# Attention softmax split between ScalarE and VectorE: a five-bank score ring, VectorE's scores in side banks, PV of two key tiles at a time, more slots for P, and an instruction order built with a price for tiling-mode changes

## Chip, cores, metric

One core of a Trainium2 chip. The metric is the device time of one execution in microseconds (us); lower is better. A span is what the profile covers of an execution, some 2 us less than its time.

## The reference

Layer norm, then self-attention times a gated feed-forward network (FFN), plus a residual. All inputs are bf16; 2048 positions, width 448, 16 heads of 28, FFN width 1792.

```python
xn = _layernorm(x)
qkv = (xn @ wqkv).reshape(B, S, 3, H, Dh) ...            # H = 16, Dh = 28
p = softmax(einsum("bhqd,bhkd->bhqk", q, k) * Dh**-0.5)  # 16 x 2048 x 2048 exponentials
s = einsum("bhqk,bhkd->bhqd", p, v) ... @ wo
g = silu(gelu(xn @ w1 + b1) @ w2 + b2)
out = x + s * g
```

The scores are cut into 1024 tiles of 128 keys x 512 queries, 64 for each of 16 blocks (a block is one group of four heads and one quarter of the queries). Each tile needs an exponential of 512 columns.

## The kernel before

A builder in Python runs its own list of tasks and fixes, before anything is compiled, the order of every engine's instructions. For each task it has a duration, and it picks the task that can start first by its own reckoning. The chip then follows that order; only semaphores, not the reckoning, decide the times.

Scores go from TensorE into a ring of six PSUM banks, in units of three (two in the first block). ScalarE takes the exponential of a whole unit in one instruction and writes bf16 tiles P to SBUF; PV multiplies P by V. For some tiles VectorE does the exponential instead, with a conversion out of the bank and three polynomial steps in SBUF. Before, such a tile is the last of its ring unit, so the unit leaves ScalarE two banks:

```python
UNITS = [range(m, m + 2) ...] + [_seq[i:i + 3] ...]      # ring units
ms = UNITS[u][:-1] if K.pick_late(u) else UNITS[u]       # VectorE takes the last one
...
def fexp(eng, b0=b0, p0=p0, n=n):                        # ScalarE
    return eng.activation(K.P[:, p0:p0 + n, :], K.ring[:, b0:b0 + n, :], ACTF.Exp, scale=SM_SCALE)
...
yield _Task(DVE, ... eng.tensor_scalar(ysb, K.ring[:, RB[m], :], ...))   # VectorE, then three steps:
yield _Task(DVE, ... eng.scalar_tensor_tensor(u, lo, EXP_A, lo, op0=ALU.add, op1=ALU.mult))
yield _Task(DVE, ... eng.scalar_tensor_tensor(u, u, EXP_B, u, op0=ALU.add, op1=ALU.mult))
yield _Task(DVE, ... eng.scalar_tensor_tensor(pl, u, EXP_K, y, op0=ALU.mult, op1=ALU.add))
# [cut]
```

One bank (`misc`) is the side bank for all other products, one (`acc`) collects PV. In the middle of the run stands GELU: ScalarE changes its table, reads 35 FFN tiles that VectorE has put into SBUF before (`p_f1`) and 21 directly from the ring (`p_direct`), and changes the table back.

```python
yield ("until", lambda: K.exp_u >= GU and K.n_f1 == len(SBT))   # GELU: all 35 must be there
```

Whether VectorE takes a tile is decided by two tables for the 16 blocks, `THS` (how much work VectorE may have waiting) and `SLACKS` (how far past the end of the block's exponentials its work may reach). P has 21 slots. When TensorE would be busy less than 85% of the last 3.4 us by its reckoning, the builder adds groups of three warming matmuls that add zero to `acc`.

## Time and profile before

| | before |
|---|---|
| time, us: median at first (3 runs) | 475.94 |
| span of the profiled execution | 474.0 |
| ScalarE busy | 462.4 (98%) |
| VectorE busy | 379.2 (80%) |
| TensorE matmuls busy | 435.4 (92%), 145 warming groups of three among them |
| exponentials on ScalarE | 231 of three banks, 118 of two, 1 of one |
| tiles on VectorE | 94 |

ScalarE is the engine without a gap; TensorE's 92% includes warming work, and the ends of its matmuls are modelled in the trace. The lines are in the prediction below.

### The profile page before, as it was taken

To read this page: it belongs to the slowest core of one execution; us is meant where nothing else is said; L and a number is where in the kernel's file an instruction comes from. 1 tells how busy PE (TensorE), PEld (TensorE's weight loads), DVE (VectorE), ACT (ScalarE), POOL (GpSimd) and SP (SyncE) were. 2 spreads that over 40 slices of the span, in tenths; PEclk is the share of its full clock that TensorE was granted. 3 is DMA by queue.
4 is the path that set the end of the run, shared out by engine and by line. 5 is a ranking of instruction groups with operands and counts; after the bars stand their busy time and mean duration, and the time that the engine had idled before them with its cause. 6 is when DMAs were issued, how large, how long until landed. Compare 5 with 4: busy or idle time off the path is not lost.

```text
span 474.0 us, 9973 instructions
## 1 busy us (share of the span) xinstructions
PE 435.4 (92%) x4150; PEld 164.0 (35%) x4185; DVE 379.2 (80%) x550; ACT 462.4 (98%) x394; POOL 39.7 (8%) x78
## 2 busy tenths in 40 slices
PE   6999999999989898989989989999999999999995
PEld 4443333333322333332223442233333333332453
DVE  8946979889885978898895939895785969899875
ACT  6999999999999999999999999999999999999994
POOL 7370001000100001000100000000100101010001
PEclk9999999999999999999999999999999999999999
DMA  8401000000000000000300000000010101011011
GB/s 268 136 8 30 2 1 0 1 1 3 1 1 0 1 1 1 1 2 21 117 1 0 1 1 1 1 1 1 1 40 2 39 1 40 1 59 39 23 41 40
DMA packets 8287, 11.08 MB, mean 23 GB/s; under 512 B 1649, under 2 KB 6897, under 8 KB 8242
## 3 DMA queue, kind: packets, MB, share of 16 engines
q1 hardware_dynamic: 7954, 9.75, 6.6%
q8 instruction: 33, 0.54, 0.5%
q10 hardware_dynamic: 288, 0.69, 0.4%
q14 instruction: 12, 0.10, 0.1%
HBM read 8.61 MB, written 1.84 MB: 22 GB/s over the span
## 4 chain that ended last, share of the span: by engine, by line
ACT 43%; PE 38%; issue 13%; DVE 4%; DMA 1%; ACTq 0%; DVEq 0%
ACT P L1195 41%; PE ring L1156 11%; PE acc L1389 7%; PE misc L1092 5%; PE misc L1034 4%; PE acc L884 2%; PE misc L722 2%; ACT h L1071 2%; PE ring L1034 2%; PE misc L1480 1%; PE misc L976 1%; DMA x_sb<-in_A_x_dram 1%; PE ring L722 1%; PE ring L976 1%; DVE kT L1331 0%
## 5 line engine op out<-in xcount | busy, mean ns | idle before, releaser
L1195 ACT ACTIVATE P<-ring 128x1536 bf16<-128x1536 f32 (+1 forms) x350 | 420.5, 1467 | 0.6 <-PE ring L1156 0.3
L1156 PE MATMUL ring<-qT,kT 32*128 32x512 bf16 (+2 forms) x1144 | 136.4, 359 | 22.0 <-ACT P L1195 16.3
L1389 PE MATMUL acc<-P,vaug 128*32 128x512 bf16 (+2 forms) x1055 | 95.9, 362 | 0.3 <-issue 0.3
L1218 DVE TENSOR_SCALAR x_sb<-ring 128x512 f32<-128x512 f32 x86 | 59.2, 688 | 26.8 <-PE ring L1156 25.9
L1156 PEld LDWEIGHTS ring<-qT,kT 32*128 32x128 bf16 x1144 | 35.6, 91 | 130.0 <-ACT P L1195 119.7
L1092 PE MATMUL misc<-w,h 128*128 128x448 bf16 x224 | 51.7, 355 | 0.2 <-DVE w L1097 0.2
L1453 POOL CAST rhi<-rc 128x16 bf16<-128x16 f32 x15 | 10.4, 692 | 394.5 <-DVE rc L1451 296.1
L1389 PEld LDWEIGHTS acc<-P,vaug 128*32 128x32 bf16 x1055 | 24.8, 93 | 50.8 <-issue 45.1
L884 PE MATMUL acc<-ident,zero 128*128 128x128 bf16 x435 | 40.4, 221 | 0.0
L1034 PE MATMUL misc<-xnT,w 128*128 128x512 bf16 x128 | 36.2, 382 | 1.4 <-issue 0.8
L1017 DVE CAST h<-misc 128x512 bf16<-128x512 f32 x35 | 24.1, 688 | 10.8 <-PE misc L1034 10.6
L1331 DVE SCALAR_TENSOR_TENSOR kT<-x_sb 128x1024 f32<-128x1024 uint16 (+1 forms) x28 | 32.0, 1141 | 0.7
L884 PEld LDWEIGHTS acc<-ident,zero 128*128 128x128 bf16 x435 | 25.1, 97 | 20.5 <-issue 19.0
L1332 DVE SCALAR_TENSOR_TENSOR kT<-kT 128x1024 f32<-128x1024 f32 (+1 forms) x28 | 31.9, 1138 | 0.4
L1331 DVE SCALAR_TENSOR_TENSOR w<-x_sb 128x1024 f32<-128x1024 uint16 (+1 forms) x22 | 25.7, 1168 | 0.4
L1332 DVE SCALAR_TENSOR_TENSOR w<-w 128x1024 f32<-128x1024 f32 (+1 forms) x22 | 25.8, 1171 | 0.2
L1092 PEld LDWEIGHTS misc<-w,h 128*128 128x128 bf16 x224 | 17.5, 97 | 23.7 <-issue 11.5
L1034 PE MATMUL ring<-xnT,w 128*128 128x512 bf16 x82 | 19.7, 380 | 0.8 <-ACT h L1071 0.6
L1334 DVE SCALAR_TENSOR_TENSOR x_sb<-kT,x_sb 128x1024 uint16<-128x1024 f32 (+1 forms) x16 | 19.0, 1187 | 0.2
L1071 ACT ACTIVATE h<-h 128x2560 bf16<-128x2560 bf16 (+2 forms) x8 | 16.6, 2073 | 0.0
L733 DVE TENSOR_SCALAR kT<-misc,ecol 128x512 bf16<-128x512 f32 x13 | 9.7, 748 | 8.3 <-PE misc L722 8.1
L1334 DVE SCALAR_TENSOR_TENSOR x_sb<-w,x_sb 128x1024 uint16<-128x1024 f32 (+1 forms) x14 | 16.0, 1142 | 0.1
(158 smaller groups left out, 425.9 us busy)
## 6 DMA issues: line engine op xcount, KB each, us to landing
h<-in_A_x_dram SPq DMA_DIRECT2D x4, 448.0 KB, 3.3
w<-in_B_w_dram SPq DMA_DIRECT2D x1, 1568.0 KB, 7.1
w<-in_B_w_dram SPq DMA_DIRECT2D x1, 1344.0 KB, 8.7
out_dram<-h SPq DMA_DIRECT2D x6, 224.0 KB, 1.9
x_sb<-in_A_x_dram SPq DMA_DIRECT2D x2, 448.0 KB, 5.2
h<-in_A_wqkv_dram SPq DMA_DIRECT2D x3, 168.0 KB, 4.8
x_sb<-in_A_x_dram ACTq DMA_DIRECT2D x1, 448.0 KB, 4.4
out_dram<-h SPq DMA_DIRECT2D x4, 112.0 KB, 1.7
```

The source lines that it names most:

```text
L884: ins = eng.matmul(K.acc[:, 0:128], K.zero[:, :], K.ident[:, :], start=False, stop=True, skip_group_check=True)
L1017: yield _Task(DVE, lambda eng: eng.tensor_copy(dst, bank), [tok], wr, 0.69, 0.0, 2)
L1034: ins = eng.matmul(bank, K.w1[:, kt, ft * 128:(ft + 1) * 128], K.xnT[:, kt, c * 512:(c + 1) * 512], start=(kt == 0), stop=(kt == KT - 1))
L1071: yield _Task(ACT, lambda eng, dst=dst, src=src: eng.activation(dst, src, ACTF.Gelu_apprx_tanh), rd, K.b_hf[c][f0:f0 + n] + ([K.b_h[c]] if ...
L1092: ins = eng.matmul(ps, hv[:, ft, t * 128:(t + 1) * 128], K.w2[:, ft, :], start=(ft == 0), stop=(ft == FT - 1))
L1156: return eng.matmul(K.ring[:, RB[m], col:col + nq], K.kT[32 * j:32 * j + 32, g, t * 128:(t + 1) * 128], K.qT[32 * j:32 * j + 32, g, c * 51 ...
L1195: return eng.activation(K.P[:, p0:p0 + n, :], K.ring[:, b0:b0 + n, :], ACTF.Exp, scale=SM_SCALE)
L1218: yield _Task(DVE, lambda eng, m=m, i=i, half=half: eng.tensor_scalar(K.ysb[i][:, 512 * half:512 * half + 512], K.ring[:, RB[m], :], SM_SC ...
L1331: yield _Task(DVE, lambda eng: eng.scalar_tensor_tensor(u, lo, EXP_A, lo, op0=ALU.add, op1=ALU.mult), ty, [tu], d, 0.0, 4)
L1332: yield _Task(DVE, lambda eng: eng.scalar_tensor_tensor(u, u, EXP_B, u, op0=ALU.add, op1=ALU.mult), [tu], [tu], d, 0.0, 4)
L1334: yield _Task(DVE, lambda eng: eng.scalar_tensor_tensor(pl.bitcast(dt.uint16), u, EXP_K, y, op0=ALU.mult, op1=ALU.add), ty + [tu], [K.b_pl ...
L1389: return eng.matmul(K.acc[32 * j:32 * j + 32, q0:q0 + nq], K.vaug[:, t, 4 * g + j, :], ap[:, col:col + nq], tile_position=(0, 32 * j), sta ...
```

## The change

The intent: relieve ScalarE of more tiles. The ring becomes five banks (units of three and two in turn) and the bank saved becomes a second side bank. VectorE's scores go to a side bank, in one group of matmuls with a ring unit's. PV takes two key tiles (eight tiles of P) at once. Free parts of `h` and `xnT` become extra P slots (42 in all before GELU, 36 after). The builder's durations are set to nearer values, and a change between full, row-tiled and column-tiled matmuls costs 0.1 us in it. The diff, cut to its core:

```diff
-        for u in range(NU):
-            ms = UNITS[u]
+        while K.next_m < MTOT:
+            b0 = 4 * (u % 2)
+            n = 2 if b0 or K.next_m < 64 else 3
+            ms = list(range(K.next_m, min(K.next_m + n, MTOT)))
+            r, K.res = K.res, None                       # a side bank reserved for VectorE
+            if r and ... and K.pick(1):
+                r["m"] = K.next_m
+                at[r["m"]] = r["bank"]
+                yield K.t_score(ms + [r["m"]], at, toks + [r["tok"]], 1)
 ...
+        self.pslots += [(hx(2, 5, 9), k) for k in range(9)] + [(hx(3, 0, 12), k) for k in range(12)]
+        self.pslots += [(self.xnT..., k) for k in range(16)]
 ...
-        for q in range(MTOT // 4):
-            ms = list(range(4 * q, 4 * q + 4))
+        for q in range(0, MTOT // 4, 2):
+            ms = list(range(4 * q, 4 * q + 8))
 ...
+SWITCH = 0.1
+        if t.E == PE and t.mode != self.pe_mode:
+            s += SWITCH
-        return _Task(PE, f, ..., [tok], 0.5, 0.12, prio)
+        return _Task(PE, f, ..., [tok], 0.432, 0.17, prio)
 ...
-SLACKS = (2.0, 2.0, 6.0, 2.0, -1.0, 2.0, 2.0, 2.0, 2.0, 1.0, 2.0, 2.0, 2.0, 4.5, 2.0, 2.0)
+SLACKS = (9.0, 9.0, 9.0, 9.0, 8.5, 9.0, 7.0, 6.5, 6.5, 9.0, 9.5, 9.0, 8.5, 9.0, 9.0, 9.0)
# [cut: the other durations, THS, bookkeeping]
```

## The prediction

> **What bounds the kernel now.** I read the page of the kernel before from the top: busy shares, the row of slices, the chain that ended last, then the groups of instructions.
>
> ```profile
> PE 435.4 (92%) x4150; PEld 164.0 (35%) x4185; DVE 379.2 (80%) x550; ACT 462.4 (98%) x394; POOL 39.7 (8%) x78
> ...
> ACT  6999999999999999999999999999999999999994
> ...
> PEclk9999999999999999999999999999999999999999
> ...
> ACT 43%; PE 38%; issue 13%; DVE 4%; DMA 1%; ACTq 0%; DVEq 0%
> ...
> L1195 ACT ACTIVATE P<-ring 128x1536 bf16<-128x1536 f32 (+1 forms) x350 | 420.5, 1467 | 0.6 <-PE ring L1156 0.3
> ```
>
> ScalarE is busy 462.4 of 474.0 us, and 350 exponentials (L1195) are 420.5 of that. Their idle time is 0.6 us. The chain names PE for 38% and issue for 13%, but that is a hand-to-hand of two engines in which PE nearly always arrives early. The list of waits says so:
>
> ```profile
> PEld ring L1156 <- ACT P L1195: 119.7, 292, 0.9
> PEld acc L1389 <- issue: 45.5, 183, 0.4
> ```
>
> 292 times the score matmuls waited for ScalarE to hand a bank back, 0.41 us on average; ScalarE waited for scores once, 0.3 us. So ScalarE sets the pace from the first exponential to the last. The table by stretches confirms it: apart from the first 12.8 us and the last 7 us only the stretch at 255 (two table loads, GELU) leaves a little idle time.
>
> ```profile
> 0.00:12.80 12.80, 8.14 (x68) 5.59 (x69) 10.98 (x40) 8.33 (x22) 9.45 (x29) 1.00 0.86 262
> ...
> 43.00:150.00 107.00, 99.25 (x929) 35.63 (x938) 90.57 (x123) 107.00 (x89) 3.57 (x8) 1.00 0.01 1
> ...
> 255.00:284.00 29.00, 26.57 (x177) 11.53 (x177) 19.53 (x24) 28.59 (x19) 1.30 (x2) 1.00 0.00 1
> ...
> 374.00:467.00 93.00, 88.39 (x1114) 36.77 (x1112) 76.46 (x113) 93.00 (x77) 2.99 (x6) 1.00 0.08 28
> 467.00:474.00 7.00, 2.31 (x25) 0.89 (x25) 3.47 (x7) 0.84 (x2) 2.06 (x2) 1.00 0.15 49
> ```
>
> The fourth busy column is ScalarE (107.00 of 107.00 us). The price of one exponential I take from the timeline, because a record's mean (1467 ns) includes its overlap with the one before. Four answers, two of each width, with start, length and count:
>
> ```profile
> 454.45 3.04 ACT L1195 ACTIVATE P<-ring 128x1536 bf16<-128x1536 f32 x2
> 454.45 9.75 ACT L1195 ACTIVATE P<-ring 128x1536 bf16<-128x1536 f32 x7
> 13.75 1.01 ACT L1195 ACTIVATE P<-ring 128x1024 bf16<-128x1024 f32 x1
> 13.75 11.14 ACT L1195 ACTIVATE P<-ring 128x1024 bf16<-128x1024 f32 x12
> ```
>
> Five three-bank exponentials took 9.75 - 3.04 = 6.71 us, 1.342 each. Eleven two-bank ones took 10.13 us, 0.921 each (some 0.004 of it waits). That is 0.427 us a tile plus 0.064 for each instruction.
>
> **What the Trainium skill says.** "ScalarE: Activation LUTs", section "What ACT_TABLE_LOAD costs", gives an ACTIVATE with immediate scale 186 ns + 0.833 ns an element and lets back-to-back ones overlap by 93 ns, so some 93 ns fixed. The slope agrees (0.427 us for 512); the fixed part here is smaller, 0.064 us, and the trace decides. "TensorE: Matmul & The Clock Gate", "Part 3: Packing small matmuls — row/col tiling", says that matmuls on different row groups run together at about 4 ns more for each. The trace agrees: the timeline has three scores at once in 0.39 us, one lasts 0.384. So a fourth score in a group is almost free. "TensorEngine Tiling (Array Packing)", "Key Properties": a change of tiling mode drains TensorE. The second line of the waits above fits: 183 times, 0.25 us each, nothing visible but issue stood ahead of PV's weight loads. "PSUM — Partial Sum Buffer", "Terms": two engines on one bank and quadrant at once is an error, so a score can be written only to a bank that its reader has given back; no error run here shows it, but every ring wait above is of that kind.
>
> **The change part by part.** I counted instructions in the two compiled programs; no time is taken from there.
>
> First, the ring: two units of three banks become three and two in turn, and the sixth bank joins the side banks. Exponentials before: 231 of three banks, 118 of two, one of one (930 tiles). After: 171 of three, 202 of two (917 tiles). There are 1024 tiles, so VectorE takes 107 and not 94. On ScalarE before: 231 x 1.342 + 118 x 0.921 + 0.50 = 419.2 us (the page has 420.5). After: 171 x 1.342 + 202 x 0.921 = 415.5. Thirteen tiles fewer would save 13 x 0.447 = 5.8, but 23 more instructions at 0.064 and other rounding give about 2 back. Net -3.7 us. ScalarE is saturated, so this comes off the span if nothing makes it wait. The GELU instructions, table loads and tanh are the same in both programs.
>
> Second, VectorE: 13 tiles more. A tile costs 0.688 (bank to SBUF, the row of L1218) and half of three 1.217 steps (rows L1331 to L1334), 2.51 us. With the singles counted exactly it is 32.5 us, so 379.2 becomes 411.7, or 87% of a 473 us span. It lies beside ScalarE. Its scores no longer take a bank out of a ring unit: before, 86 of the 94 did.
>
> Third, TensorE: a VectorE score rides in a ring unit's group (saving a switch), and PV handles eight tiles instead of four. In program order, mode changes fall from 871 to 800 and PV runs from 223 to 132. At 0.25 us each some 15 us may be freed, but TensorE is not the bound; the program spends the room on warming matmuls (684 instead of 435, the L884 row). Worth 0 on the path.
>
> Fourth, more room for P: free parts of the h and xnT tiles serve as slots. ScalarE never waited for a slot before, so it only pays for VectorE's later finishes at the end of a block. Worth 0.
>
> Fifth, the tail. The last PV is now 32 small matmuls in place of 16 after the last exponential. The chain shows 16 as 0.34 us, so +0.3 us; the epilogue after it has the same instructions.
>
> Sixth, new waits. While ScalarE works on a two-bank unit, TensorE has 0.92 us to refill the three banks; a three-bank unit gives 1.34. Pairing each refill with its exponential in the trace before (86 two-bank windows in the main part), the fill begins a median 0.06 us after the bank comes free, a tenth begin later than 0.2 to 0.3 us, the latest 0.61. A fill takes 0.39, and must end some 0.15 before ScalarE's turn, so up to 0.37 us of delay is free. After, there are 170 such windows in place of 86, and a PV block in the way is longer (eight tiles are two rounds of 0.21 us, with extra tiles three). If one window in ten is late by a tenth to two tenths: 17 x 0.15 = 2.5; but PV blocks are fewer and the order was built with closer durations, so I take 0.8 as an estimate.
>
> Sum: 475.9 - 3.7 + 0.3 + 0.8 = 473.3; since the reordering may also remove some of the 1 us of small waits of before, I put it at 472.9 us.
>
> **The rivals.** (a) Two-bank windows too short: TensorE's other work (projections in pairs of 0.43 us, PV of 0.45 to 0.67) lands just before refills and ScalarE waits. For it: the first stage before, all two-bank and thick with projections, holds the 0.30 us wait. Against it: 292 early arrivals. If 50 windows lose 0.15 us, +7 us, 479. (b) VectorE becomes the bound of a stage: at 87% with 107 tiles, block ends wait for its last polynomial, then side banks, FFN matmuls and P slots back up. Against it: the extra slots, and the FFN's first products that must be ready for GELU are done in the program order about two blocks ahead, where before the last ended at 254.6, just before GELU at 255.4. If it bites: +3 to +10 us. (c) A larger gain, since FFN and PV work no longer delays scores. Against it: ScalarE's idle time in the loop was under 1 us, so there is nothing to win there; only 470 is reachable. (d) A hole around GELU, where the ring takes the sixth bank back and slots shrink to 21: 0.5 to 2 us.
>
> **Range and chances.** The floor is 475.9 - 3.7 - 1.5 (all waits gone) = 470.7, the upper side is (a) or (b) in a mild form. Eight in ten: 470.5 to 476.5. Two per cent faster is 466.4, below the floor: chance 0.02. Two per cent slower is 485.5, which needs a full failure of (a) or (b): 0.03.
>
> **What would show it right or wrong.** Right: ScalarE's exponentials total 415 to 417 us busy, its idle time before them stays under 3 us, VectorE near 412, and the last stretch after the final exponential is 0.3 us longer. (a) shows as idle time of ScalarE released by the score line, mostly ahead of three-bank units; (b) as ScalarE or score waits on VectorE, or PV waiting on the last polynomial; (d) as a gap between 245 and 290. I am wrong if the exponentials' price per bank changes, or if the clock of TensorE falls below 1.00.

## The result, and the profile after

| | before | after |
|---|---|---|
| time, us: median (lowest to highest, runs) | 476.46 (475.87 to 477.20, 4) | 472.90 (472.84 to 472.99, 4) |
| span | 474.0 | 471.2 |
| ScalarE's exponentials, busy us | 420.50 | 417.38 |
| tiles on VectorE | 94 | 107 |

The ratio is 0.9925 (95% interval 0.9907 to 0.9942): 0.75% faster. Here and below a ratio is the mean time of one kernel's fast runs over that of the other's fast runs of the same rounds, so not quite the ratio of the medians.

The kernel before has two levels within the fast state: in the later rounds some six in ten of its runs are near 475.9 (granted clock mostly 0.997 to 1.000), the others near 476.9 (mostly 0.994 to 0.995). Two of its four runs here, 476.98 and 477.20, are of the upper level. Against the lower one the change is worth 3.0 us, or 0.63%.

From the page of the changed kernel: the busy row, ScalarE's slices, TensorE's clock, and the chain.

```profile
PE 439.9 (93%) x4407; PEld 175.2 (37%) x4440; DVE 408.6 (87%) x581; ACT 459.1 (97%) x417; POOL 42.5 (9%) x78
...
ACT  6999999999999999999999999999999999999994
...
PEclk9999999999999999999999999999999999999999
...
PE 46%; ACT 39%; issue 13%; DVE 1%; ACTq 0%; DVEq 0%
```

ScalarE is still the engine without a gap, with 3.3 us less to do. VectorE has taken 29.4 us more. The chain now names TensorE for 46%, again as the partner of a hand-to-hand: its list of waits shows who was early.

```profile
PEld ring L1158 <- ACT P L1217: 68.9, 172, 0.9
PEld ring L1158 <- ACT h L1217: 38.0, 86, 1.0
...
PEld ring L1158 <- ACT xnT L1217: 22.8, 56, 0.7
PEld acc L1417 <- issue: 22.7, 93, 0.4
```

Together 314 times and 129.7 us in which the score matmuls waited for ScalarE; `h` and `xnT` are P tiles in the extra slots. The unexplained issue before PV's weight loads has halved (45.5 us before), as PV runs are fewer. ScalarE's own waits, of the same kernel:

```profile
ACT h L1217 <- PE acc L1417: 0.7, 1, 0.7
...
ACT P L1217 <- PE ring L1158: 0.6, 2, 0.3
```

The first is new in kind: an exponential waited for PV to free its P slot, at the end of the third block. The stretch around GELU, in the table by stretches (fourth busy column ScalarE), has no hole:

```profile
255.00:284.00 29.00, 28.33 (x191) 11.88 (x186) 22.93 (x27) 28.95 (x19) 1.37 (x2) 1.00 0.00 1
```

**An account that holds for every run.** I took three figures from each trace. "List" is the sum of the exponentials at 1.343 us (three banks), 0.917 (two) and 0.49 (one); 1.343 and 0.917 are the distances from end to end of successive instructions where none waits. "Waits" is the sum of what those distances exceed that by (a one-bank instruction's own excess is left out), and of ScalarE's idle time before its GELU instructions. "Tail" runs from ScalarE's last instruction to the end of the span. What remains of the span, the start, GELU and the tanh, should be the same in all.

| run | list | waits | tail | span | rest |
|---|---|---|---|---|---|
| before | 418.9 | 1.8 | 6.2 | 474.0 | 47.1 |
| after | 414.9 | 3.4 | 6.1 | 471.2 | 46.8 |
| late94 | 420.8 | 3.2 | 6.3 | 477.0 | 46.7 |
| before_more | 414.2 | 20.3 | 6.8 | 488.6 | 47.3 |
| before_post | 417.2 | 1.8 | 6.9 | 473.2 | 47.3 |
| noroom | 412.6 | 26.6 | 6.2 | 492.4 | 47.0 |
| pv1 | 415.8 | 3.3 | 6.1 | 472.2 | 47.0 |
| sw0 | 415.4 | 38.4 | 7.0 | 507.4 | 46.6 |
| oldcost | 414.0 | 10.8 | 6.7 | 478.8 | 47.3 |
| ring4 | 419.1 | 7.4 | 8.7 | 481.8 | 46.6 |
| nodum | 414.9 | 9.4 | 7.1 | 477.9 | 46.5 |
| pool | 413.5 | 9.2 | 6.3 | 475.8 | 46.8 |
| best | 413.5 | 8.8 | 6.0 | 475.1 | 46.8 |
| best2 | 412.6 | 6.1 | 6.3 | 471.6 | 46.6 |

The rest lies between 46.5 and 47.3 in all fourteen, so list, waits and tail are where every difference below lies, within 0.8 us. List and waits add up to the time of the exponentials by their definition; what the table tests is whether the rest stays, and the price: the medians of the distances lie at 1.343 to 1.344 us and 0.915 to 0.917 in every run but sw0, where the three-bank ones have 1.482. Before to after: list -4.0, waits +1.6, tail -0.1, rest -0.3.

### The profile page after: what moved, and what is told of

Its sections match the earlier page's. It is cut to its first block, busy times and chain, and to the rows that moved or that the text cites.

```text
span 471.2 us, 10607 instructions
## 1 busy us (share of the span) xinstructions
PE 439.9 (93%) x4407; PEld 175.2 (37%) x4440; DVE 408.6 (87%) x581; ACT 459.1 (97%) x417; POOL 42.5 (9%) x78
## 4 chain that ended last, share of the span: by engine, by line
PE 46%; ACT 39%; issue 13%; DVE 1%; ACTq 0%; DVEq 0%
ACT P L1217 23%; PE ring L1158 12%; ACT h L1217 9%; PE acc L1417 7%; ACT xnT L1217 6%; PE ring L1028 5%; PE acc L878 4%; PE ring L1087 4%; PE misc L1087 3%; PE misc L716 2%; PE ring L716 2%; PE ring L970 1%; PE misc L1028 1%; PE acc L860 1%; PE misc L970 1%
## 5 line engine op out<-in xcount | busy, mean ns | idle before, releaser
L1217 ACT ACTIVATE P<-ring 128x1024 bf16<-128x1024 f32 x210 | 237.8, 1305 | 0.6 <-PE ring L1158 0.6
L1217 ACT ACTIVATE h<-ring 128x1536 bf16<-128x1536 f32 (+1 forms) x97 | 111.3, 1292 | 1.0 <-PE acc L1417 0.7
L1217 ACT ACTIVATE xnT<-ring 128x1536 bf16<-128x1536 f32 x66 | 77.6, 1350 | 0.0
L1262 DVE TENSOR_SCALAR x_sb<-misc 128x512 f32<-128x512 f32 x64 | 44.0, 688 | 8.8 <-PE misc L1158 7.8
L1417 PE MATMUL acc<-P,vaug 128*32 128x512 bf16 (+2 forms) x587 | 50.0, 357 | 0.3 <-DVE x_sb L1350 0.3
L1262 DVE TENSOR_SCALAR x_sb<-ring 128x512 f32<-128x512 f32 x43 | 29.6, 688 | 12.6 <-PE ring L1158 12.5
L1348 DVE SCALAR_TENSOR_TENSOR kT<-kT 128x1024 f32<-128x1024 f32 (+1 forms) x32 | 37.8, 1183 | 0.4
L1087 PE MATMUL ring<-w,h 128*128 128x448 bf16 x140 | 33.9, 355 | 0.0
L1348 DVE SCALAR_TENSOR_TENSOR w<-w 128x1024 f32<-128x1024 f32 (+1 forms) x24 | 27.6, 1150 | 0.1
L1158 PE MATMUL misc<-qT,kT 32*128 32x512 bf16 (+1 forms) x66 | 24.6, 377 | 0.2 <-DVE w L1092 0.2
L1417 PE MATMUL acc<-h,vaug 128*32 128x512 bf16 x239 | 24.0, 384 | 0.0
L1087 PE MATMUL misc<-w,h 128*128 128x448 bf16 x84 | 20.0, 355 | 0.0
```

The lines of the kernel that those rows point to most:

```text
L1087: ins = eng.matmul(ps, hv[:, ft, t * 128:(t + 1) * 128], K.w2[:, ft, :], start=(ft == 0), stop=(ft == FT - 1))
L1158: return eng.matmul(dst, K.kT[32 * j:32 * j + 32, g, t * 128:(t + 1) * 128], K.qT[32 * j:32 * j + 32, g, c * 512 + q0:c * 512 + q0 + nq], ...
L1217: return eng.activation(reg[:, i0:i0 + n, :], K.ring[:, b0:b0 + n, :], ACTF.Exp, scale=SM_SCALE)
L1262: yield _Task(DVE, lambda eng, i=i, half=half, bank=bank: eng.tensor_scalar(K.ysb[i][:, 512 * half:512 * half + 512], bank, SM_SCALE * LOG ...
L1348: yield _Task(DVE, lambda eng: eng.scalar_tensor_tensor(u, u, EXP_B, u, op0=ALU.add, op1=ALU.mult), [tu], [tu], d, 0.0, 4)
L1417: return eng.matmul(K.acc[32 * j:32 * j + 32, q0:q0 + nq], K.vaug[:, t, 4 * g + j, :], ap[:, col:col + nq], tile_position=(0, 32 * j), sta ...
```

## The experiments

All twelve gave correct results. Times are medians; "before" ran beside each at 475.9 to 476.0. The changed kernel was not run again beside them, so differences from its 472.90 are between rounds.

### 1. Is the gain VectorE's thirteen tiles, and only that? (late94)

The changed kernel with a cap on VectorE's tiles.

```diff
-        if not 0 < sub < NBLK or r < 4:
+        if not 0 < sub < NBLK or r < 4 or sum(x // 64 == m // 64 for x in K.late) >= (12 if m // 64 == 9 else 6):
```

> The changed kernel with VectorE's tiles capped at six a block (twelve in the GELU block): 94 as in the kernel before, in place of 107. Theory A (the gain is ScalarE's shorter list of exponentials and nothing else): 173 three-bank, 205 two-bank and one one-bank exponentials make 173 x 1.343 + 205 x 0.917 + 0.49 = 420.8 us in place of 414.9, so about 5.9 us slower than the changed kernel, 478.5 to 479, which is 2 us slower than the kernel before. Theory B (the new order of TensorE's work, PV of two key tiles and side banks are worth something by themselves): at most 475.

478.87 us, ratio to before 1.0064 (1.0049 to 1.0079). Theory A. With the tiles of before, the new ring, side banks, PV in pairs and order together are 3 us slower than before: by the account 1.9 of list, since 3 + 2 banks need more instructions (379 against 350) than 3 + 3 with two now and then, and 1.4 of waits. By the account the list grew 5.9 us against the changed kernel and nothing else moved by more than 0.2.

### 2. Could the old layout have carried as many? (before_more, before_more_room, before_post)

The kernel before with a larger slack, in all blocks, and then only in the blocks after GELU:

```diff
 NU = len(UNITS)
+SLACKS = tuple(x + 2.0 for x in SLACKS)                              # before_more
+SLACKS = SLACKS[:10] + tuple(x + 2.0 for x in SLACKS[10:])            # before_post
```

> The kernel before with every block's slack for VectorE raised by 2: 105 VectorE tiles instead of 94 in the old six-bank ring, exponentials 220 x 1.343 + 129 x 0.917 + 0.49 = 414.2 us against 418.9. Theory A1 (any ring can carry that many; it is only a matter of the settings): 471.5. Theory A2 (the single side bank of the old layout makes the FFN's first products late for GELU once VectorE has more to do before it): a hole of ScalarE of 5 us or more just before the direct GELU reads, time 480 to 490. Theory A3 (too few P slots, 21): ScalarE waits for PV all over the blocks' ends, time above 476.

490.72 us, ratio 1.0316 (1.0299 to 1.0334), with 105 tiles, 0.7 us above the range of theory A2. ScalarE's waits and its timeline name one hole (columns of the timeline: start, length, instruction, idle time before it and its releaser):

```profile
ACT h L1072 <- PE ring L1035: 18.6, 1, 18.6
```

```profile
261.57 1.91 ACT L1072 ACTIVATE h<-h 128x2048 bf16<-128x2048 bf16 x1
282.12 1.45 ACT L1072 ACTIVATE h<-ring 128x1536 bf16<-128x1536 f32 x1 [18.64 <-PE ring L1035]
```

In the hole VectorE still had six of the 35 FFN tiles to fetch, at 266.6, 272.0, 273.8, 275.6, 277.5 and 279.3, each by way of the single side bank, taking turns with the last VectorE scores and their polynomials:

```profile
275.63 0.69 DVE L1018 CAST h<-misc 128x512 bf16<-128x512 f32 x1
277.46 0.69 DVE L1018 CAST h<-misc 128x512 bf16<-128x512 f32 x1 [1.13 <-PE misc L1035]
279.28 0.69 DVE L1018 CAST h<-misc 128x512 bf16<-128x512 f32 x1 [1.13 <-PE misc L1035]
```

That is theory A2, as far as late FFN tiles go. That the one side bank made them late is not shown: in the first 12.9 us of the hole VectorE itself was nearly always busy (third busy column), and only the last two fetches above waited for TensorE to fill the bank again.

```profile
263.50:276.40 12.90, 11.83 (x140) 8.48 (x140) 12.62 (x15) 0.00 (x0) 0.00 (x0) 1.00 0.00 1
```

Theory A3 (P slots) is out for this layout with these tables: ScalarE waited for PV nowhere. A run that gave the old layout the new slots was refused, for a race: an exponential would have written into `xnT` while a late projection still read it.

> The same with the changed kernel's extra P slots (42 before GELU, 36 after it) put into the kernel before. Theory A3 (slots) expects the waits gone and 471 to 472. Theory A2 (FFN's first products late for GELU) expects no change against the run without the slots, within 0.5 us.

> The kernel before with VectorE's slack raised by 2 only in the blocks after GELU: 98 VectorE tiles in place of 94, exponentials 227 x 1.343 + 122 x 0.917 + 0.49 = 417.2 us in place of 418.9. Theory A (the old layout is held back only by the FFN's first products that must be done before GELU; after GELU it can carry more): 1.7 us faster than before, ratio 0.9965. Rival (the old six-bank ring cannot take more anywhere, since VectorE's scores hold a ring bank): no gain or slower.

before_post: 475.04 us, ratio 0.9977 (0.9968 to 0.9986), 98 tiles. After GELU the old layout does take more: the list fell by 1.7 and the waits stayed at 1.8. A tail longer by 0.7 us ate half of the gain. So before GELU the old layout, with its tables, was at its limit because the 35 FFN tiles had to be ready; in the kernel before the last was fetched at 254.6, just before the table load at 255.4. The changed kernel, with two side banks, had fetched its last at 217.8, as the summary of that line's instructions shows (lowest, median and highest duration in ns, then the times of the first and the last):

```profile
L1011 DVE CAST h<-ring x16: 681/691/693, 102.9 to 217.8; 128x512 bf16<-128x512 f32 x16
```

Whether the second bank does it, or the new order, the tables or the slots, no run isolates: with one side bank the changed builder never finished its list, so there is no run of it.

### 3. Are the extra P slots worth nothing? (noroom)

```diff
-        K.pon += [(NP, 9), (NP + 9, 12)]
-        K.pon.append((NP + 21, 15))
```

> The changed kernel without the extra P slots (21 all the time). The settings then give 112 VectorE tiles and exponentials of 170 x 1.343 + 201 x 0.917 = 412.6 us, 2.3 less than in the changed kernel. My prediction gave the slots no worth of their own: 470.5 to 472. The rival (the large slacks let PV of a block's end lie some 9 us behind, and with 21 slots ScalarE must wait for PV at nearly every block's end): 480 to 490, with ScalarE idle released by PV's accumulation.

494.10 us, ratio 1.0382 (1.0367 to 1.0398). The rival, and 4 us beyond its range. ScalarE's waits, and the weight load of PV that ended the longest of them:

```profile
ACT P L1217 <- PE acc L1415: 22.6, 13, 6.0
```

```profile
107.42 0.11 PEld L1415 LDWEIGHTS acc<-P,vaug 128*32 128x32 bf16 x5 [0.42 <-DVE x_sb L1348]
```

Thirteen times, up to 6.0 us at once, ScalarE could not write because PV had not read a slot; in the longest wait PV itself was held up by a last polynomial step of VectorE (L1348) at the end of a block, and the large slacks let these steps lie behind. With these slacks the changed kernel needs the slots; smaller slacks with 21 slots were not tried.

### 4. PV of one key tile at a time (pv1)

```diff
-        for q in range(0, MTOT // 4, 2):
-            ms = list(range(4 * q, 4 * q + 8))
+        for q in range(0, MTOT // 4, 1):
+            ms = list(range(4 * q, 4 * q + 4))
-                hole = cnt[m % 4] < 2
+                hole = cnt[m % 4] < 1
```

> The changed kernel with PV of one key tile (four scores) at a time, as before. The settings then give 105 VectorE tiles: exponentials 171 x 1.343 + 203 x 0.917 = 415.8 us, 0.9 more than in the changed kernel. Theory A (TensorE has room, PV's grouping is worth nothing by itself): 473.5 to 474.3. Theory B (the mode changes saved by PV in pairs keep TensorE in time for the short windows): ScalarE's waits for scores grow by 2 us or more, 475.5 or slower.

474.07 us, ratio to before 0.9953 (0.9936 to 0.9970), inside theory A's 473.5 to 474.3. The list grew 0.9 us (VectorE got 105 tiles), the waits are 3.3 against 3.4 and the tail is the same. So the grouping of PV is worth nothing by way of waits, although pv1 changes mode 860 times and the changed kernel 800 (counted in the traces' weight loads). Its 1.2 us come from the two tiles that the builder then withholds from VectorE; whether other tables would give them back was not tried.

### 5. The order and the price of a mode change (sw0, oldcost)

sw0 takes the price away and keeps the new, shorter durations. oldcost goes back to the old table of durations as a whole.

```diff
-SWITCH = 0.1
+SWITCH = 0.0
# oldcost, besides: projections 0.432 -> 0.5, FFN 0.378 -> 0.42, scores 0.218 + ... -> 0.17 + 0.05 n,
# PV of up to eight 0.446 -> 0.6, more than eight 0.84, no side-by-side start of row groups, and so on
```

> The changed kernel with its order built as if a change of tiling mode cost nothing (the 0.1 us set to 0; the rest as it is). 106 VectorE tiles: exponentials 171 x 1.343 + 202 x 0.917 + 0.49 = 415.4 us, 0.5 more. The order now holds 536 warming groups in place of 228, as the builder thinks TensorE idle more often. Theory A (ScalarE's list decides, TensorE arrives early whatever the order): 473 to 474.5. Theory B (a wrong order puts warming and other work ahead of refills, some 0.1 us each in 170 short windows): waits of ScalarE for scores grow by 3 to 10 us, 476 to 483.

> The changed kernel with its order built with the whole old table of durations (no price for a mode change, but the old durations, which are padded: 0.5 us for a projection pair in place of 0.43, 0.36 for a PV group). 109 VectorE tiles, 170 three-bank, 202 two-bank and one one-bank exponential: 414.0 us against 414.9. Theory A (what counts is that the sum of durations is not below the real one; padding does the job of the mode price, and the run without a mode price failed only since its durations had just been cut): 471 to 475. Theory B (the builder must know where the mode changes are): ScalarE's waits above 6 us, 477 or slower.

sw0: 509.48 us, ratio 1.0698 (1.0682 to 1.0713). This went beyond even theory B's range. The expectation that TensorE arrives early "whatever the order" is false. In its waits the score matmuls waited for ScalarE only 34 + 15 + 7 times (314 in the changed kernel), stood 142 times behind issue, and ScalarE waited for them; two of the three lines for ScalarE's hand-backs and the main one of ScalarE's own:

```profile
PEld ring L1158 <- issue: 54.9, 142, 0.4
PEld ring L1158 <- ACT P L1217: 12.8, 34, 0.5
ACT P L1217 <- PE ring L1158: 11.8, 37, 0.8
PEld ring L1158 <- ACT h L1217: 6.1, 15, 0.4
```

The order held 536 warming groups in place of 228, because the builder thought TensorE idle; by theory B they fill what the mode changes really take. In the page's group row they are 1608 matmuls with 42.4 us of issue before their weight loads:

```profile
L878 PE MATMUL acc<-ident,zero 128*128 128x128 bf16 x1608 | 123.9, 220 | 0.0
...
L878 PEld LDWEIGHTS acc<-ident,zero 128*128 128x128 bf16 x1608 | 92.3, 98 | 48.0 <-issue 42.4 <-DVE x_sb L1262 0.2
```

How much of the 38 us of waits is misplaced warming and how much misplaced real work was not separated. oldcost: 480.74 us, ratio 1.0085 (1.0066 to 1.0103), waits 10.8: theory B by its line of 6 us, and slower than the kernel before. It has 237 warming groups, near the 228 of the changed kernel, so their number does not explain it. In its profile the granted clock was 0.50 from 422.1 to 428.9 us, and ScalarE was idle for 3.1 us there; the other 7.7 us are still above 6. Padding helps a good deal (38 to 11 us of waits) but did not replace the nearer durations with the price of a mode change; the two were not separated further.

### 6. A four-bank ring: the price of an instruction and of a short window (ring4)

```diff
-            n = 2 if b0 or K.next_m < 64 else 3
+            n = 2
```

> The changed kernel with a four-bank ring: all units have two banks, two ring banks are side banks. 110 VectorE tiles, 457 two-bank exponentials: 457 x 0.917 = 419.1 us, 4.2 more than the 414.9 of the changed kernel although ScalarE has three tiles fewer. Theory A (a fixed 0.064 us for each of 84 more instructions decides, less three tiles): 476.5 to 479, the rest above 477.1 being waits in the windows, which are now all short. If instructions cost nothing beyond their tiles: 471.6.

483.67 us, ratio 1.0157 (1.0142 to 1.0172). By the account 4.2 us more list, as expected, though ScalarE had three tiles fewer; and the list's price holds, for the median distance of its 457 two-bank exponentials is again 0.917; so an instruction does cost its 0.064 or so. But 4.0 us more waits and a tail longer by 2.6 put it above the expected 479. With all windows 0.92 us the waits doubled, in small pieces: its profile names only seven waits of exponentials for the score line, 2.2 us in all; by subtraction the rest is in longer records.

### 7. Fewer warming matmuls (nodum)

```diff
-HAM_WIN, HAM_LOW, DUM = 3.4, 0.85, 0.17
+HAM_WIN, HAM_LOW, DUM = 3.4, 0.5, 0.17
```

> The changed kernel with the threshold for warming matmuls lowered from 0.85 to 0.5 of a window: 53 warming groups in place of 228, the same exponentials (202 and 171). Theory A (they lie in TensorE's idle time and ScalarE sets the pace; real work keeps the clock up): within 1 us of 472.9, granted clock 1.00. Theory B (they stand in the way of refills): ScalarE's waits in the loop fall from 1.6 us to under 0.8, 471.5 to 472. Theory C (they hold the clock up): granted clock below 0.97 and slower than 475.

480.83 us, ratio 1.0102 (1.0069 to 1.0135). Theory C: the granted clock fell, to 0.952 to 0.964 on average in the four runs, and the waits grew by 6.0 us (in the profiled one, 479.67, the fastest).

```profile
PEclk9999999999999989998999989999999979989898
```

The Trainium skill, "TensorE: Matmul & The Clock Gate", "Part 1: The HAM clock gate (the "warmup" mystery)", says that a monitor sets the clock of TensorE's array by how busy it has been lately, in windows of about 3.4 us. The trace agrees: between the first and the last exponential lie six stretches of 3.4 or 6.8 us (30.7 in all) at a granted clock of 0.50, and in the 3.4 us ahead of each TensorE was busy 50 to 63% (93% in the changed kernel as a whole). The last of the six in the table by stretches, where the granted clock stands behind the five busy columns:

```profile
440.00:446.80 6.80, 6.49 (x61) 4.00 (x64) 4.17 (x6) 5.50 (x5) 0.00 (x0) 0.50 0.01 2
```

In the six ScalarE was idle for 4.9 us together, so most of the 6.0 us of new waits are where the clock was halved; that the other order made none of them is not shown. The order held 53 warming groups (159 matmuls in its page's groups) in place of 228, so the 175 left out, which I had called a way of spending spare room, were worth 8 us. One such stretch may also be what parts the two levels of the kernel before: 0.003 to 0.004 of 474 us is 1.4 to 1.9 us of clock, and half of 3.4 us is 1.7 (an estimate from these numbers; no trace of the upper level was kept).

### 8. A version that beats both? (pool, best, best2)

If VectorE's time limits its tiles, SBUF-only work can go to GpSimd, which is 9% busy: q squared, the gate's product, and the residual add of three query blocks.

```diff
-  _Task(DVE, ... eng.tensor_tensor(qs, qb, qb, ALU.mult), ..., 0.43, ...)
+  _Task(POOL if g > 0 else DVE, ... (the same), 1.15 if g > 0 else 0.43, ...)
-  _Task(DVE, ... eng.scalar_tensor_tensor(g_sb, sg, 1.0, fb, op0=ALU.add, op1=ALU.mult), ..., 0.63, ...)
+  _Task(POOL, ... eng.tensor_tensor(g_sb, sg, fb, ALU.mult), ..., 1.05, ...)
+  _Task(POOL, ... eng.tensor_tensor(g_sb, g_sb, fb, ALU.add), ..., 1.05, ...)
-  _Task(DVE, ... eng.tensor_tensor(o, o, K.x2[...], ALU.add), ..., 0.4, ...)
+  _Task(POOL if c < C - 1 else DVE, ... (the same), 1.05 if c < C - 1 else 0.4, ...)
# best: the same, THS and SLACKS set anew. best2: durations 1.4 to 1.55 on GpSimd, polynomial steps x 1.08 after GELU, tables set anew
```

> The changed kernel with three kinds of SBUF-only work moved from VectorE to the idle GpSimd (q squared from the second head group on, the gate's product, the residual add of three of the four query blocks), the same settings. 110 VectorE tiles in place of 107: 170 x 1.343 + 202 x 0.917 = 413.5 us in place of 414.9. Theory A (VectorE's time is what limits the number of its tiles, and a tile is worth 0.447 us of ScalarE): 1.4 us faster, 471.5. Rival (the two engines get in each other's way at SBUF, VectorE's instructions become longer and the order slips): 473 or slower, with VectorE's three polynomial steps longer than 1.217 us.

> The same with the two tables of thresholds and slacks set anew for it. 110 VectorE tiles, the same 170 and 202 exponentials, 413.5 us. If the waits in the loop (1.6 us more than in the kernel before) shrink too: 470 to 471.5. If the retuned tables only fit the builder's model: no better than the run with the old tables, 471.5 to 473.

> The version with work on GpSimd once more, the order now built with the durations that the two runs before measured (GpSimd's steps 1.4 to 1.55 us in place of 1.05 to 1.15, VectorE's polynomial steps after GELU 8 per cent longer), thresholds set anew. 112 VectorE tiles: 170 x 1.343 + 201 x 0.917 = 412.6 us, 2.3 less than in the changed kernel. Theory A (the earlier loss came from an order built on durations that were too short): waits back to 3 to 4 us, 470.5 to 472. Rival (the slow-down of VectorE beside GpSimd comes and goes with the moment, so no fixed duration in the builder fits, and waits stay above 6 us): 473 or slower.

pool 477.84 (1.0037; 1.0022 to 1.0052), best 474.26 (0.9961; 0.9950 to 0.9973), best2 473.49 (0.9945; 0.9932 to 0.9957). None beats the changed kernel, whose ratio is 0.9925; best2 comes within 0.6 us of its median, and their intervals overlap. pool is in the rival's range; best is in neither of its two, but slower than both. The list did shrink (by 1.4, 1.4 and 2.3), but the waits grew more. A reason that fits is in VectorE's groups of pool: the polynomial steps after GELU (`kT`), when GpSimd works beside them, against the same steps before it (`w`), and (last line) against the same steps after GELU in the changed kernel:

```profile
L1349 DVE SCALAR_TENSOR_TENSOR kT<-kT 128x1024 f32<-128x1024 f32 x31 | 42.1, 1358 | 0.3
L1348 DVE SCALAR_TENSOR_TENSOR kT<-x_sb 128x1024 f32<-128x1024 uint16 x31 | 40.4, 1304 | 2.0 <-DVE rc L1488 0.2
...
L1349 DVE SCALAR_TENSOR_TENSOR w<-w 128x1024 f32<-128x1024 f32 x21 | 25.6, 1219 | 0.0
```

```profile
L1347 DVE SCALAR_TENSOR_TENSOR kT<-x_sb 128x1024 f32<-128x1024 uint16 x30 | 36.7, 1223 | 1.8
```

1.30 to 1.36 us against 1.22, while GpSimd's steps took 1.40 to 1.54 us where the two steps of that kind and width in the kernel before took 1.03. The Trainium skill, "SBUF — State Buffer", "Who interferes with whom", says that a VectorE instruction with two SBUF inputs and a GpSimd instruction that reads SBUF contend for a read port that they share; that fits. With the measured means and new tables in the builder (best2) the waits came down from 9.2 to 6.1 us, not to 3.4: the rival, if only just. The tables alone may have done as much. The profile of best is of its slowest execution (476.90 us, median 474.26), in which the clock was 0.50 for two stretches, 10.2 us in all, and ScalarE idle for 2.9 us of them; at the median its waits would be some 6 us too (an estimate, 8.8 less the difference of 2.6).

## Why the prediction came out as it did

The time was right, 472.9 us. By the spans the change is -2.8 us where the terms add up to -3.0. Step by step:

- **What bounds the kernel.** Right. ScalarE sets the pace in both kernels, and the account closes on its list and its waits. The price was put together loosely: 1.342 and 0.921 give 0.421 us a tile and 0.079 an instruction, not the 0.427 and 0.064 used. The medians of all distances, 1.343 and 0.917, give 0.426 and 0.065, so the figures used were good.
- **First, the ring.** -3.7 predicted; the list shrank by 4.0 and the busy time by 3.1. The 0.3 are the 0.004 of waits in the two-bank price, on 84 more such instructions. late94 shows that without the thirteen tiles there is no gain but a loss of 3 us. What I did not say is what kept the old layout from having them: before_more shows FFN tiles that were not ready at GELU.
- **Second, VectorE.** 411.7 predicted, 408.6 measured, 87% as said. I added lengths of records to a busy time that counts overlaps once: the records' lengths grew by 32.0 us (403.8 to 435.8, summed from the traces), as reckoned, but busy time by 29.4.
- **Third, TensorE, "worth 0 on the path".** Right for PV's waits (pv1). At 0.25 us the 71 mode changes are 17.8 us, not 15; the time that PV's weight loads stood behind issue fell by 22.8. Wrong for what I called spending the room: the warming matmuls hold the clock (nodum, 8 us).
- **Fourth, P slots, "worth 0".** Wrong as a statement about the part. Against a kernel that has the new slacks they are worth 21 us (noroom). I looked for a wait in the kernel before and found none; but the slots pay for a setting that the change brings with it.
- **Fifth, the tail, +0.3.** It came out 0, and pv1, whose last PV is 16 matmuls again, has the same tail. The last PV did grow, from 0.37 to 0.59 us in the chain. But before, three matmuls of the output projection (0.74 us) stood between the last exponential and the last PV; after, three follow the PV, and four that stand ahead of it end 0.2 us after the exponential.
- **Sixth, waits, +0.8, with about 0.4 off for small waits removed.** Net +1.6 measured. The estimate of 2.5 that I first worked out and then shaded down was nearer. By the distances, two-bank exponentials lost 0.9 us in both kernels, but three-bank ones 0.5 before and 2.5 after: 15 of 171 came over 0.05 us late, 2.3 us together. One of them is the slot wait (0.7 us), which I had ruled out; the others fit rival (a) in a mild form, ahead of three-bank units as said. In return GELU no longer has the wait of 0.35 us that it had before.
- **The rest**, -0.3, was not predicted; the first exponential ends 0.36 us earlier.

The errors of the last three and of the first nearly cancelled (-0.3, -0.4, +1.2, -0.3), which is why the sum looks better than its terms; so close a hit is luck. Of the signs that I named, idle time under 3 us, the clock and the price held; the exponentials' 417.4 us busy are just above the 415 to 417, VectorE is 3 us below its 412, and the longer tail did not come. The rivals: (b) did not occur but for the one slot wait, (d) did not, and (c) could not. Against (a) I had put 292 early arrivals of TensorE. They were early in that order: with the mode price gone, and 308 more warming groups in the order, the waits grew by 35 us (sw0). A wait list describes one order and says nothing of another one.

## What to carry to other kernels

Where one engine is saturated, write the span as its list of instructions, plus its waits, plus the ends; here that account closed within 0.8 us over fourteen kernels, and each part of a change could be placed in its terms. A part of a change that is "worth nothing" by the profile of before may be what another part needs, so ask of each part what breaks without it. In an order fixed beforehand, look for what the builder's durations leave out: a tenth of a microsecond at each of some 800 mode changes made 35 us of waits here, over ten times what the change gained.

## What the Trainium skill lacked or had wrong

- "ScalarE: Activation LUTs", "What ACT_TABLE_LOAD costs": by its figures (186 ns less 93 ns of overlap) back-to-back exponentials have some 93 ns of fixed cost each. From PSUM to SBUF with an immediate scale the runs show some 65 ns (1.343 us for 1536 columns and 0.917 us for 1024, so 0.426 us for 512).
- "TensorEngine Tiling (Array Packing)", "Key Properties": it says that a change of mode drains TensorE, but not what that costs. Here PV's weight loads stood 0.25 us behind issue on average (45.5 us in 183 times), partly while earlier matmuls still ran, and an order built without any price for it ran 7.0% slower than the kernel before.
- "SBUF — State Buffer", "Who interferes with whom": it names two sizes, of measurements in opposite issue orders, but none for a mixed stream. Here VectorE's two-input steps of 1024 columns became 7 to 11% longer on average in the two groups shown, and GpSimd's steps some 36 to 50%.
